# Halving the units of the weighted values, adding four of them by DMA, and copying attention weights with one DMA per chunk

## The chip, the cores and the metric

One core of a Trainium2 chip runs the kernel. The metric is the device time of one execution in microseconds (us), the median over several runs. A profiled run also has a span, from its first to its last recorded instruction, which is about 2 us shorter than the time. A run counts as slow when it is over 1.5% above the fastest of its kernel, and as fast otherwise; all comparisons below are between fast runs. In one group of rounds a single run of the kernel before was slow (218.4 us, granted clock 0.76); it enters no ratio. The granted clock is the share of full speed at which the chip let the tensor engine run. A DMA "lands" when the last of its sixteen completions is recorded.

## The reference, cut to what matters

```python
# A: local attention. 2048 tokens, 512 features, 32 heads of 16, 8 positions at distance 0, 2, ..., 14
logits = einsum("bhsd,bhswd->bhsw", q, kg) * scale        # 8 logits for each token and head
attn   = softmax(where(mask, logits, -1e9))
o      = einsum("bhsw,bhswd->bhsd", attn, vg)             # the weighted values
a      = o.reshape(B, S, D) @ wo
# B: a token mixer: layernorm, then two matrix products over the tokens, with a gelu between
b      = (gelu(layernorm(x)^T @ w1 + b1) @ w2 + b2)^T
out    = g * a + (1 - g) * b                              # g = sigmoid(x . gate_w)
```

The weighted values are the part that changes: for each of 2048 x 512 outputs, 8 products and 7 additions, elementwise, on the vector engine (DVE), while the tensor engine (PE) computes part B beside it. The projection with `wo` needs the weighted values and is added into the same PSUM banks as the last product of B.

## The kernel before

The kernel records operations in a small scheduler, which fixes the order of each engine's instructions before the launch; engines then run in that order and wait on semaphores. `A(engine, function, duration, ...)` records an operation, `tt` is one DVE instruction over two tensors, `sch.dma` is one DMA, and `prio` and the durations only steer the order.

Attention weights of one half of the tokens lie in `ATT[h]`: 128 partitions = 4 chunks of 256 tokens x 32 heads. The weighted values need them on 128 partitions = 32 heads x 4 groups of the head's features. So each chunk (32 partitions of 4 KB) is copied four times, to every fourth partition, by four DMAs of 128 KB:

```python
for c in range(4):
    for dhi in range(4):
        src = psub(ATT[h], 32 * c, 32, 0, [(1, NW * UT_)])
        dst = bass.AP(AVW[h].tensor, AVW[h].offset + dhi * pst + c * NW * UT_, [[4 * pst, 32], [1, NW * UT_]])
        prev = sch.dma("pool", ..., 131072, ds, issue=1.0, reads=["att%d" % h], writes=["avw%d_%d_%d" % (h, c, dhi)] + al, ...)
```

Then eight units of 256 tokens: one product of 8192 elements a partition, and three additions that halve it to 1024:

```python
for u in range(8):
    h, c = u // 4, u % 4
    pv = PV[1 if u % 2 == 0 else 0]                       # two buffers
    A("dve", tt(pv, <values>, <weights of chunk c>, ALU.mult), 4.42, ..., name="avm%d" % u)
    A("dve", tt(pv[:, 0:4], pv[:, 0:4], pv[:, 4:8], ALU.add), 2.28, ..., name="ava%d" % u)
    A("dve", tt(pv[:, 0:2], pv[:, 0:2], pv[:, 2:4], ALU.add), 1.22, ..., name="avb%d" % u)
    avl = A("dve", tt(OT[:, u], pv[:, 0], pv[:, 1], ALU.add), 0.68, ..., name="avc%d" % u)
```

The end of the kernel is a row of sixteen output tiles of 128 tokens. Each takes 14 matmuls of part B, four of the projection (`wo`, which reads `OT`), an eviction on ScalarE (ACT) that needs the small vectors `OMG` (a reciprocal on DVE) and `C2`, and a DMA out. The projections trail by five tiles.

Of the kernel before, what the change touches and what calls it, by code (L numbers as in the profile page):

```python
# [8 lines left out]
ALU = mybir.AluOpType  # L9
AF = mybir.ActivationFunctionType  # L10
# [3 lines left out]
D = 512  # L14
NH = 32
DH = 16
NW = 8
# [290 lines left out]
def bass_gated_mix__sliding_local_dilated__mixer_token_mlp__prompt_kernel(nc, A_x, A_wqkv, A_wo, B_x, B_w1, B_b1, B_w2, B_b2, gate_w, out, dbg=None):  # L308
    with contextlib.ExitStack() as es:
# [128 lines left out]
        def sub(ap_, offs, dims):  # L438
            return bass.AP(ap_.tensor, ap_.offset + offs, [list(ap_.ap[0])] + [list(d) for d in dims])

        def psub(ap_, p0, np_, offs, dims):
            pst = ap_.ap[0][0]
            return bass.AP(ap_.tensor, ap_.offset + p0 * pst + offs, [[pst, np_]] + [list(d) for d in dims])

        def tt(o_, a_, b_, op_):
            return lambda e: e.tensor_tensor(out=o_, in0=a_, in1=b_, op=op_)  # L446

        def act(o_, i_, f_, **kw):
            return lambda e: e.activation(out=o_, in_=i_, func=f_, **kw)  # L449
# [99 lines left out]
        def PE(fn, dur, reads, writes, name, prio=0):  # L549
            op = A("pe", fn, dur, reads=reads, writes=writes, after=([chain[0]] if chain[0] is not None else []), name=name, prio=prio)  # L550
            chain[0] = op
            return op
# [174 lines left out]
        for h in range(2):  # L727
            for pr in range(2):
                bb = PLAN[h][pr]
                for k_ in range(2):  # L730
                    dl = 2 * pr + k_
                    for s_, n_ in (((0, 512), (512, 512)) if h == 0 else ((0, HS),)):
                        sbs = [2 * h + x_ for x_ in range(s_ // 512, (s_ + n_) // 512)]
                        A("dve", tt(sub(PB[bb[k_]], s_, [(HS, NW), (1, n_)]), sub(QH[h], dl * HS + s_, [(0, NW), (1, n_)]),
                                    sub(KH[h], dl * KR + PAD + s_, [(-2, NW), (1, n_)]), ALU.mult), 4.32 * n_ / HS + 0.1,
                          reads=["q%d_%d" % (dl, x_) for x_ in sbs] + ["k%d_%d" % (dl, x_) for x_ in sbs] + (["khalo"] if h else ["kpad"] if s_ == 0 else ["k%d_0" % dl]),
                          writes=PR[bb[k_]], name="qk%d_%d_%d" % (h, dl, s_))
                A("dve", tt(PB[bb[0]], PB[bb[0]], PB[bb[1]], ALU.add), 4.42, reads=PR[bb[1]], writes=PR[bb[0]], name="qa%d_%d" % (h, pr))
            b0, b1 = PLAN[h][0][0], PLAN[h][1][0]
            A("pe", f_sum(h, b0, b1, h == 0), 2.1 + (1.0 if h == 0 else 0), reads=PR[b0] + PR[b1] + ["rp"] + ((XTALL + ["gwrep"]) if h == 0 else []),  # L740
              writes=LGB + (["b3"] if h == 0 else []), name="sum%d" % h, prio=-100, delay=0.5)
            if h == 0:
                A("act", act(E32, ps[:, 3, :], AF.Relu, scale=-1.0, bias=ZMAX), 0.6, reads=["b3"], writes=["e32"], name="zclip")
                A("act", act(EB, E32, AF.Exp, scale=-1.0, bias=ZMAX), 0.6, reads=["e32"], writes=["eb"], name="zexp", table=LOGEXP)
            A("act", act(LOG[h], ps[:, 4:8, :], AF.Copy), 1.9, reads=LGB, writes=["log%d" % h], name="lev%d" % h, prio=-5)
            if h == 0:
                A("dve", tt(psub(LOG[0], 0, 32, 0, [(UT_, NW), (1, PAD)]), psub(LOG[0], 0, 32, 0, [(UT_, NW), (1, PAD)]), MASK, ALU.add), 0.2,
                  reads=["mask"], writes=["log0"], name="msk")
            TR = ["s4", "s2", "s1"]
            A("dve", tt(M4, LOG[h][:, 0:4, :], LOG[h][:, 4:8, :], ALU.max), 0.65, reads=["log%d" % h], writes=["s4"], name="mx4_%d" % h)  # L750
            A("dve", tt(M2, M4[:, 0:2, :], M4[:, 2:4, :], ALU.max), 0.4, reads=["s4"], writes=["s2"], name="mx2_%d" % h)
            A("dve", tt(M1, M2[:, 0, :], M2[:, 1, :], ALU.max), 0.25, reads=["s2"], writes=["s1"], name="mx1_%d" % h)
            A("dve", tt(LOG[h], LOG[h], sub(M1, 0, [(0, NW), (1, UT_)]), ALU.subtract), 1.2, reads=["s1"], writes=["log%d" % h], name="msub%d" % h)
            A("act", act(ATT[h], LOG[h], AF.Exp), 1.9, reads=["log%d" % h], writes=["att%d" % h], name="exp%d" % h, prio=-5, table=LOGEXP)
            A("dve", tt(S4, ATT[h][:, 0:4, :], ATT[h][:, 4:8, :], ALU.add), 1.2, reads=["att%d" % h], writes=["s4"], name="sm4_%d" % h)
            A("dve", tt(S2, S4[:, 0:2, :], S4[:, 2:4, :], ALU.add), 0.65, reads=["s4"], writes=["s2"], name="sm2_%d" % h)
            A("dve", tt(S1, S2[:, 0, :], S2[:, 1, :], ALU.add), 0.4, reads=["s2"], writes=["s1"], name="sm1_%d" % h)
            A("act", act(RS, S1, AF.Ln), 0.4, reads=["s1"], writes=["rs"], name="lns%d" % h, prio=-5, table=LOGEXP)
            A("dve", tt(RS, RS, E32[:, h * UT_:(h + 1) * UT_], ALU.add), 0.35, reads=["e32"], writes=["rs"], name="rsz%d" % h)
            A("act", act(RB, RS, AF.Exp, scale=-1.0, bias=ZMAX), 0.4, reads=["rs"], writes=["rb"], name="rb%d" % h, prio=-5, table=LOGEXP)  # L760
            A("dve", tt(ATT[h], ATT[h], sub(RB, 0, [(0, NW), (1, UT_)]), ALU.mult), 1.2, reads=["rb"], writes=["att%d" % h], name="nrm%d" % h)
            al = ["q%d_%d" % (dl, 2 * h + s_) for dl in range(4) for s_ in range(2)] + ["k%d_%d" % (dl, 2 * h + s_) for dl in range(4) for s_ in range(2)]
            al += ["khalo"] if h else ["kpad"]
            prev = None
            for c in range(4):
                for dhi in range(4):
                    src = psub(ATT[h], 32 * c, 32, 0, [(1, NW * UT_)])
                    pst = AVW[h].ap[0][0]
                    dst = bass.AP(AVW[h].tensor, AVW[h].offset + dhi * pst + c * NW * UT_, [[4 * pst, 32], [1, NW * UT_]])
                    ds = sch.dsem("av%d_%d_%d" % (h, c, dhi))  # L770
                    prev = sch.dma("pool", (lambda d_, s_: lambda e: e.dma_start(d_, s_))(dst, src), 131072, ds, issue=1.0,  # L771
                                   reads=["att%d" % h], writes=["avw%d_%d_%d" % (h, c, dhi)] + al, after=[prev] if prev else [],
                                   name="av%d_%d_%d" % (h, c, dhi))
                    al = []

        def f_te(e):
            ins = None
# [7 lines left out]
        A("dve", tt(C2, OMG, B2C, ALU.mult), 0.12, reads=["omg", "b2c"], writes=["c2"], name="c2")  # L785


        avl = None
        for u in range(8):
            h, c = u // 4, u % 4  # L790
            b = 1 if u % 2 == 0 else 0
            pv = PV[b]
            vr = ["v%d_%d" % (dl, sb) for dl in range(4) for sb in sorted(set([u // 2, max(0, (256 * u - PAD)) // 512]))]
            A("dve", tt(pv, sub(V5, PAD + 256 * u, [(-2, NW), (VR, 4), (1, UT_)]), sub(AVW[h], c * NW * UT_, [(UT_, NW), (0, 4), (1, UT_)]), ALU.mult), 4.42,
              reads=["avw%d_%d_%d" % (h, c, dhi) for dhi in range(4)] + vr + ["vpad"], writes=["p%d" % b], after=[avl] if avl else [], name="avm%d" % u)
            A("dve", tt(pv[:, 0:4], pv[:, 0:4], pv[:, 4:8], ALU.add), 2.28, writes=["p%d" % b], name="ava%d" % u)
            A("dve", tt(pv[:, 0:2], pv[:, 0:2], pv[:, 2:4], ALU.add), 1.22, writes=["p%d" % b], name="avb%d" % u)
            avl = A("dve", tt(OT[:, u], pv[:, 0], pv[:, 1], ALU.add), 0.68, reads=["p%d" % b], writes=["ot%d" % u, OTRES[u]], name="avc%d" % u)


        def f_ph2(ft, bank, half):
# [46 lines left out]

        def finish_tile(i):
            bank = banks[i]  # L850
            PE(f_wo(i, bank, 0, D), 0.87, ["ot%d" % (i // 2), "wo"], ["b%d" % bank], "wo%d" % i)
            A("act", act(OUTS[:, i % 4, :], ps[:, bank, :], AF.Identity, scale=col(OMG, i), bias=col(C2, i)), 0.78,
              reads=["b%d" % bank, "omg", "c2"], writes=["outs%d" % (i % 4)] + (["p2h"] if i == 0 else []), name="ev%d" % i)
            sch.dma("sp", (lambda i_: lambda e: e.dma_start(outv[:, i_, :], OUTS[:, i_ % 4, :]))(i), 131072, ds_out[i % 4], issue=0.5,
                    reads=["outs%d" % (i % 4)], name="d_out%d" % i)
# [17 lines left out]
            finish_tile(i)  # L873
        for hf, (c0, c1) in enumerate(CH):
            bank = lastb[hf]
            PE(f_wo(L, bank, c0, c1), 0.44, ["ot%d" % (L // 2), "wo"], ["b%d" % bank], "wo%d_%d" % (L, hf))
            if hf == 0:
                A("act", act(OUTS[:, 4, c0:c1], ps[:, bank, 0:256], AF.Identity, scale=col(OMG, L), bias=col(C2, L)), 0.55,
                  reads=["b%d" % bank, "omg", "c2"], writes=["outs4"], name="ev%da" % L)
# [86 lines left out]
```

## Time and profile before

171.09 us, median of three runs (170.79 to 171.18). The profiled run has a span of 168.5 us.

| | before |
|---|---|
| PE busy | 161.6 us (96%) |
| DVE busy | 151.9 us (90%) |
| first product of weighted values starts | 88.24 us |
| last addition ends | 163.9 us |
| PE idle before its last projections | 1.04 us |

The first part of the page gives each engine's busy time, share of the span and number of instructions:

```profile
span 168.5 us, 2085 instructions
PE 161.6 (96%) x835; PEld 79.4 (47%) x851; DVE 151.9 (90%) x115; ACT 73.1 (43%) x102; POOL 19.6 (12%) x57
```

Two engines are nearly full, so shares alone do not say which one ends the kernel. PE's timeline does; its columns are start, length, engine, line, operation, and in brackets the idle time ahead and what ended it. L832 is part B, L841 the projection:

```profile
156.46 3.22 PE L832 MATMUL ps<-arena 128*128 128x256 bf16 x28
159.51 3.62 PE L841 MATMUL ps<-arena 128*128 128x512 bf16 x16
164.18 1.69 PE L841 MATMUL ps<-arena 128*128 128x512 bf16 x11 [1.04 <-DVE arena L446]
```

PE runs through until 163.1 us, waits 1.04 us for DVE, and does the last twelve matmuls (one is missing from the trace). The end of the chain of waits (start, length, what) shows what DVE was doing: one unit after another, the last one here. Steps called "issue" of 0.02 us stand between the rows and are left out.

```profile
154.56 5.04 DVE arena L446 x2
159.62 2.30 DVE arena L446
161.94 1.24 DVE arena L446
163.20 0.70 DVE arena L446
163.91 0.27 issue
164.18 1.70 PE ps L841 x11
```

The groups of DVE instructions by form, from 87.2 us on (count, busy us, mean ns, idle before), give the price of each size:

```profile
L446 DVE TENSOR_TENSOR arena<-arena 128x8192 bf16<-128x8192 bf16 x8 | 35.4, 4419 | 0.9 <-DMA arena<-arena 0.9
L446 DVE TENSOR_TENSOR arena<-arena 128x4096 bf16<-128x4096 bf16 x8 | 18.3, 2290 | 0.2
L446 DVE TENSOR_TENSOR arena<-arena 128x2048 bf16<-128x2048 bf16 x10 | 12.1, 1223 | 0.3
L446 DVE TENSOR_TENSOR arena<-arena 128x1024 bf16<-128x1024 bf16 x9 | 6.2, 691 | 0.3
```

DVE's timeline where the first product starts, and the attention copies (number, length of one issue in ns, first and last start; then issue to landing):

```profile
86.92 0.25 DVE L784 RECIPROCAL arena<-arena 128x16 f32<-128x16 f32 x1
87.21 0.17 DVE L446 TENSOR_TENSOR arena<-arena 128x16 f32<-128x16 f32 x1
88.24 5.03 DVE L446 TENSOR_TENSOR arena<-arena 128x8192 bf16<-128x8192 bf16 x2 [0.85 <-DMA arena<-arena]
...
L771 POOL DMA_DIRECT2D arena<-arena x32: 511/519/535, 83.0 to 118.1; - x32
...
DMA to landing us min/median/max: 2.9/4.3/8.4
```

The first of the four DMAs of the first chunk is issued at 82.97 us, the fourth lands at 88.11 us, and DVE waited 0.85 us for it.

### The profile page before, as it was taken

The numbers are of one execution on the slowest core, as the hardware profiler recorded it, in microseconds if no ns is written. First come the engines' busy times: TensorE is split into PE (matmuls) and PEld (weight loads), VectorE is DVE, ScalarE is ACT, GpSimd is POOL, SyncE is SP. The second block draws the span as 40 slices with busy tenths as digits, with TensorE's granted clock in tenths as the row PEclk, the third lists the DMA queues.
The fourth block names the chain that finished last, engine by engine and source line by source line (L and its number), as shares of the span: only waits on it lengthen the run. The fifth ranks groups of instructions, "written<-read, shape, count | busy, mean of one in ns | idle before, by whom it ended". The sixth has DMA issues, their size and how long they took to land.

```text
span 168.5 us, 2085 instructions
## 1 busy us (share of the span) xinstructions
PE 161.6 (96%) x835; PEld 79.4 (47%) x851; DVE 151.9 (90%) x115; ACT 73.1 (43%) x102; POOL 19.6 (12%) x57
## 2 busy tenths in 40 slices
PE   6999999999989999999999999999999999999973
PEld 2865555555534444444443444444444444444732
DVE  2609999999999799999979999999999999999981
ACT  3266777666671277656215297000121111111172
POOL 7000000000000000000396000079100000000000
PEclk9999999999999999999999999999999999999999
DMA  5999999910000392995799999999900011000022
GB/s 137 271 247 252 235 321 290 302 66 6 0 0 0 110 302 63 285 286 142 215 218 288 355 275 270 290 243 207 198 31 31 31 46 51 31 31 31 31 91 96
DMA packets 43144, 26.87 MB, mean 159 GB/s; under 512 B 7552, under 2 KB 41984, under 8 KB 43136
## 3 DMA queue, kind: packets, MB, share of 16 engines
q1 hardware_dynamic: 40800, 21.96, 49.9%
q0 software_dynamic: 1632, 4.21, 10.4%
q10 hardware_dynamic: 704, 0.59, 1.1%
q8 instruction: 6, 0.10, 0.3%
q14 instruction: 2, 0.02, 0.0%
HBM read 18.88 MB, written 2.10 MB: 125 GB/s over the span
## 4 chain that ended last, share of the span: by engine, by line
PE 54%; DVE 36%; ACT 4%; issue 3%; DMA 2%; DVEq 0%
DVE arena L446 36%; PE ps L805 24%; PE ps L649 22%; ACT arena L449 3%; PE ps L590 2%; PE ps L719 2%; DMA arena<-in_A_x_dram 2%; PE ps L841 1%; PE ps L569 1%; ACT L901 1%; PE ps L713 1%; PE ps L560 1%; DVE arena L881 0%; DVEq L905 0%; PE ps L779 0%
## 5 line engine op out<-in xcount | busy, mean ns | idle before, releaser
L446 DVE TENSOR_TENSOR arena<-arena 128x8192 bf16<-128x8192 bf16 (+10 forms) x72 | 134.8, 1902 | 3.2 <-DMA arena<-arena 0.9
L832 PE MATMUL ps<-arena 128*128 128x512 bf16 (+1 forms) x234 | 50.0, 366 | 0.2
L805 PE MATMUL ps<-arena 128*128 128x512 bf16 x218 | 48.7, 379 | 1.4 <-ACT arena L449 0.8
L449 ACT ACTIVATE arena<-ps,arena 128x512 bf16<-128x512 f32 (+1 forms) x30 | 21.6, 728 | 65.2 <-PE ps L841 46.6
L449 ACT ACTIVATE arena<-ps 128x512 bf16<-128x512 f32 (+3 forms) x53 | 33.4, 649 | 20.3 <-PE ps L649 10.4
L649 PE MATMUL ps<-arena 128*128 128x512 bf16 x172 | 38.0, 379 | 0.2
L832 PEld LDWEIGHTS ps<-arena 128*128 128x128 bf16 x238 | 23.3, 98 | 25.3
L805 PEld LDWEIGHTS ps<-arena 128*128 128x128 bf16 x224 | 21.5, 98 | 28.2 <-ACT arena L449 1.8
L649 PEld LDWEIGHTS ps<-arena 128*128 128x128 bf16 x176 | 19.8, 113 | 17.7
L771 POOL DMA_DIRECT2D arena<-arena x32 | 16.4, 517 | 98.3 <-DVE arena L446 98.3
L688 DVE BATCH_NORM_STATS2 arena<-arena 128x6 f32<-128x512 bf16 x16 | 10.0, 682 | 7.5 <-DMA arena<-in_A_x_dram 7.5
L841 PE MATMUL ps<-arena 128*128 128x512 bf16 (+1 forms) x66 | 15.5, 366 | 1.1 <-DVE arena L446 1.0
L901 ACT ACT_TABLE_LOAD x9 | 11.5, 1283 | 2.4 <-issue 2.3
L841 PEld LDWEIGHTS ps<-arena 128*128 128x128 bf16 x68 | 6.6, 98 | 8.2 <-DVE arena L446 1.3
L449 ACT ACTIVATE arena<-arena 128x16 f32<-128x16 f32 (+5 forms) x10 | 6.8, 679 | 5.2 <-DVE arena L446 5.1
L702 DVE TENSOR_SCALAR arena<-arena 128x512 bf16<-128x512 bf16 x16 | 5.3, 413 | 0.0
L590 PE MATMUL ps<-arena 128*128 128x256 bf16 x32 | 3.8, 273 | 0.0
L719 PE MATMUL ps<-arena 128*32 128x512 bf16 x64 | 3.8, 380 | 0.0
L590 PEld LDWEIGHTS ps<-arena 128*128 128x128 bf16 x32 | 3.4, 114 | 0.4 <-DVE arena L580 0.4
L543 PE MATMUL ps<-arena 128*128 128x512 bf16 x5 | 2.3, 628 | 1.1 <-POOL arena L455 1.1
L719 PEld LDWEIGHTS ps<-arena 128*32 128x32 bf16 x64 | 1.6, 97 | 1.9 <-issue 0.4
L881 DVE TENSOR_SCALAR arena<-ps,arena 128x256 bf16<-128x256 f32 x1 | 0.5, 544 | 2.0 <-PE ps L841 2.0
(36 smaller groups left out, 15.3 us busy)
## 6 DMA issues: line engine op xcount, KB each, us to landing
arena<-in_B_w_dram SPq DMA_DIRECT2D x7, 1024.0 KB, 8.3
arena<-in_B_w_dram SPq DMA_DIRECT2D x8, 896.0 KB, 7.9
arena<-arena POOLq DMA_DIRECT2D x32, 128.0 KB, 4.3
out_dram<-arena SPq DMA_DIRECT2D x15, 128.0 KB, 1.7
arena<-in_A_x_dram SPq DMA_DIRECT2D x3, 512.0 KB, 4.3
arena<-in_A_wqkv_dram SPq DMA_DIRECT2D x2, 512.0 KB, 5.9
arena<-in_A_wo_dram SPq DMA_DIRECT2D x1, 512.0 KB, 8.7
arena<-in_A_x_dram SPq DMA_DIRECT2D x2, 128.0 KB, 3.4
```

Of the source, the lines that this page charges most:

```text
L446: return lambda e: e.tensor_tensor(out=o_, in0=a_, in1=b_, op=op_)
L449: return lambda e: e.activation(out=o_, in_=i_, func=f_, **kw)
L590: ins = e.matmul(ps[:, dl, hb * 256:hb * 256 + 256], lhsT=sub(WQKV, dt * 3 * D + dl, [(4, 128)]), rhs=XT[:, dt, hb * 256:hb * 256 + 256], ...
L649: ins = e.matmul(ps[:, bank, :], lhsT=sub(WQKV, dt * 3 * D + tn * D + dl, [(4, 128)]), rhs=XT[:, dt, sb * 512:(sb + 1) * 512], start=(dt = ...
L688: A("dve", (lambda t_: lambda e: e.bn_stats(out=ST6[:, t_, :], in_=X[:, t_, :]))(t), 0.67, reads=["x%d" % t], writes=["st%d" % t], name="s ...
L702: A("dve", (lambda t_: lambda e: e.tensor_scalar(out=X[:, t_, :], in0=X[:, t_, :], scalar1=col(RSTD, t_), scalar2=col(NMR, t_), op0=ALU.mu ...
L719: ins = e.matmul(ps[32 * c:32 * c + 32, 4 + wp, :], lhsT=RP, rhs=sub(PB[b_], 2 * wp * HS + c * UT_, [(HS, 2), (1, UT_)]), start=(k_ == 0), ...
L771: prev = sch.dma("pool", (lambda d_, s_: lambda e: e.dma_start(d_, s_))(dst, src), 131072, ds, issue=1.0, reads=["att%d" % h], writes=["av ...
L805: ins = e.matmul(ps[:, bank, :], lhsT=W1W[:, (ft // 2) % 3, st, 128 * (ft % 2):128 * (ft % 2) + 128], rhs=X[:, st, :], start=(st == 0), st ...
L832: ins = e.matmul(ps[:, bank, 0:c1 - c0], lhsT=W2S[i // 2][:, ft, 128 * (i % 2):128 * (i % 2) + 128], rhs=UT[:, ft, c0:c1], start=(ft == 0) ...
L841: ins = e.matmul(ps[:, bank, 0:c1 - c0], lhsT=OT[:, i // 2, dl, 128 * (i % 2):128 * (i % 2) + 128], rhs=WO[:, dl, c0:c1], start=False, sto ...
L901: e.preload_act_table_set(want)
```

## The change

Its intent: units of 128 tokens in four buffers, so that DVE can start a unit while another is still being reduced; for four of the sixteen units the first, largest addition is taken from DVE and done by a DMA that accumulates into SBUF; and one DMA per chunk in place of four for the attention copies. The softmax operations get a stronger priority, which keeps their place in the order.

```diff
-                for dhi in range(4):
-                    src = psub(ATT[h], 32 * c, 32, 0, [(1, NW * UT_)])
-                    dst = bass.AP(AVW[h].tensor, AVW[h].offset + dhi * pst + c * NW * UT_, [[4 * pst, 32], [1, NW * UT_]])
-                    prev = sch.dma("pool", ..., 131072, ds, issue=1.0, ...)
+                src = psub(ATT[h], 32 * c, 32, 0, [(0, 4), (1, NW * UT_)])
+                dst = sub(AVW[h], c * NW * UT_, [(1, NW * UT_)])
+                prev = sch.dma("pool", ..., 524288, sch.dsem("av%d_%d" % (h, c)), issue=1.0, ...)
 ...
-        for u in range(8):                # product 4.42, additions 2.28, 1.22, 0.68, in two buffers
+        AVD = (6, 8, 10, 12)
+        def av_mult(i):                   # four buffers: slot = i % 4
+            AV(tt(pv, <values>, <weights>, ALU.mult), 2.27, ...)
+            if i in AVD:
+                sch.dma("pool", ... e.dma_start(pw(0, 4), pw(4, 4), accum_op=ALU.add), 1500000, ..., name="avd%d" % i)
+        def av_add(i):
+            if i not in AVD:
+                AV(tt(pw(0, 4), pw(0, 4), pw(4, 4), ALU.add), 1.14, ...)
+            AV(tt(pw(0, 2), pw(0, 2), pw(2, 2), ALU.add), 0.62, ...)
+            AV(tt(<OT of 128 tokens>, pw(0, 1), pw(1, 1), ALU.add), 0.36, ...)
+        for i in range(16):               # a unit added by DMA is finished on DVE two units later
+            av_mult(i); ...
 ...
-            PE(f_wo(i, bank, 0, D), 0.87, ["ot%d" % (i // 2), "wo"], ...)
+            PE(f_wo(i, bank, 0, D), 0.87, ["ot%d" % i, "wo"], ...)
 ...           (and prio=-30 on the softmax operations)
```

PE, ACT and SP keep their order of instructions. On DVE the order of the weighted values changes, and `C2`, which stood right behind the reciprocal, moves to the middle of the units.

More of the change, by code (lines that the diff above doesn't have):

```diff
@@ L744, in bass_gated_mix__sliding_local_dilated__mixer_token_mlp__prompt_kernel @@
                 A("act", act(EB, E32, AF.Exp, scale=-1.0, bias=ZMAX), 0.6, reads=["e32"], writes=["eb"], name="zexp", table=LOGEXP)
-            A("act", act(LOG[h], ps[:, 4:8, :], AF.Copy), 1.9, reads=LGB, writes=["log%d" % h], name="lev%d" % h, prio=-5)
+            A("act", act(LOG[h], ps[:, 4:8, :], AF.Copy), 1.9, reads=LGB, writes=["log%d" % h], name="lev%d" % h, prio=-30)
             if h == 0:
                 A("dve", tt(psub(LOG[0], 0, 32, 0, [(UT_, NW), (1, PAD)]), psub(LOG[0], 0, 32, 0, [(UT_, NW), (1, PAD)]), MASK, ALU.add), 0.2,
-                  reads=["mask"], writes=["log0"], name="msk")
+                  reads=["mask"], writes=["log0"], name="msk", prio=-30)
@@ L749, in bass_gated_mix__sliding_local_dilated__mixer_token_mlp__prompt_kernel @@
             TR = ["s4", "s2", "s1"]
-            A("dve", tt(M4, LOG[h][:, 0:4, :], LOG[h][:, 4:8, :], ALU.max), 0.65, reads=["log%d" % h], writes=["s4"], name="mx4_%d" % h)
-            A("dve", tt(M2, M4[:, 0:2, :], M4[:, 2:4, :], ALU.max), 0.4, reads=["s4"], writes=["s2"], name="mx2_%d" % h)
-            A("dve", tt(M1, M2[:, 0, :], M2[:, 1, :], ALU.max), 0.25, reads=["s2"], writes=["s1"], name="mx1_%d" % h)
-            A("dve", tt(LOG[h], LOG[h], sub(M1, 0, [(0, NW), (1, UT_)]), ALU.subtract), 1.2, reads=["s1"], writes=["log%d" % h], name="msub%d" % h)
@@ L754, in bass_gated_mix__sliding_local_dilated__mixer_token_mlp__prompt_kernel @@
-            A("act", act(ATT[h], LOG[h], AF.Exp), 1.9, reads=["log%d" % h], writes=["att%d" % h], name="exp%d" % h, prio=-5, table=LOGEXP)
-            A("dve", tt(S4, ATT[h][:, 0:4, :], ATT[h][:, 4:8, :], ALU.add), 1.2, reads=["att%d" % h], writes=["s4"], name="sm4_%d" % h)
-            A("dve", tt(S2, S4[:, 0:2, :], S4[:, 2:4, :], ALU.add), 0.65, reads=["s4"], writes=["s2"], name="sm2_%d" % h)
-            A("dve", tt(S1, S2[:, 0, :], S2[:, 1, :], ALU.add), 0.4, reads=["s2"], writes=["s1"], name="sm1_%d" % h)
@@ L758, in bass_gated_mix__sliding_local_dilated__mixer_token_mlp__prompt_kernel @@
-            A("act", act(RS, S1, AF.Ln), 0.4, reads=["s1"], writes=["rs"], name="lns%d" % h, prio=-5, table=LOGEXP)
-            A("dve", tt(RS, RS, E32[:, h * UT_:(h + 1) * UT_], ALU.add), 0.35, reads=["e32"], writes=["rs"], name="rsz%d" % h)
-            A("act", act(RB, RS, AF.Exp, scale=-1.0, bias=ZMAX), 0.4, reads=["rs"], writes=["rb"], name="rb%d" % h, prio=-5, table=LOGEXP)
-            A("dve", tt(ATT[h], ATT[h], sub(RB, 0, [(0, NW), (1, UT_)]), ALU.mult), 1.2, reads=["rb"], writes=["att%d" % h], name="nrm%d" % h)
+            A("dve", tt(M4, LOG[h][:, 0:4, :], LOG[h][:, 4:8, :], ALU.max), 0.65, reads=["log%d" % h], writes=["s4"], name="mx4_%d" % h, prio=-30)
@@ new lines, in bass_gated_mix__sliding_local_dilated__mixer_token_mlp__prompt_kernel @@
+            A("dve", tt(M2, M4[:, 0:2, :], M4[:, 2:4, :], ALU.max), 0.4, reads=["s4"], writes=["s2"], name="mx2_%d" % h, prio=-30)
+            A("dve", tt(M1, M2[:, 0, :], M2[:, 1, :], ALU.max), 0.25, reads=["s2"], writes=["s1"], name="mx1_%d" % h, prio=-30)
+            A("dve", tt(LOG[h], LOG[h], sub(M1, 0, [(0, NW), (1, UT_)]), ALU.subtract), 1.2, reads=["s1"], writes=["log%d" % h], name="msub%d" % h, prio=-30)
+            A("act", act(ATT[h], LOG[h], AF.Exp), 1.9, reads=["log%d" % h], writes=["att%d" % h], name="exp%d" % h, prio=-30, table=LOGEXP)
@@ new lines, in bass_gated_mix__sliding_local_dilated__mixer_token_mlp__prompt_kernel @@
+            A("dve", tt(S4, ATT[h][:, 0:4, :], ATT[h][:, 4:8, :], ALU.add), 1.2, reads=["att%d" % h], writes=["s4"], name="sm4_%d" % h, prio=-30)
+            A("dve", tt(S2, S4[:, 0:2, :], S4[:, 2:4, :], ALU.add), 0.65, reads=["s4"], writes=["s2"], name="sm2_%d" % h, prio=-30)
+            A("dve", tt(S1, S2[:, 0, :], S2[:, 1, :], ALU.add), 0.4, reads=["s2"], writes=["s1"], name="sm1_%d" % h, prio=-30)
+            A("act", act(RS, S1, AF.Ln), 0.4, reads=["s1"], writes=["rs"], name="lns%d" % h, prio=-30, table=LOGEXP)
@@ L762, in bass_gated_mix__sliding_local_dilated__mixer_token_mlp__prompt_kernel @@
+            A("dve", tt(RS, RS, E32[:, h * UT_:(h + 1) * UT_], ALU.add), 0.35, reads=["e32"], writes=["rs"], name="rsz%d" % h, prio=-30)
+            A("act", act(RB, RS, AF.Exp, scale=-1.0, bias=ZMAX), 0.4, reads=["rs"], writes=["rb"], name="rb%d" % h, prio=-30, table=LOGEXP)
+            A("dve", tt(ATT[h], ATT[h], sub(RB, 0, [(0, NW), (1, UT_)]), ALU.mult), 1.2, reads=["rb"], writes=["att%d" % h], name="nrm%d" % h, prio=-30)
             al = ["q%d_%d" % (dl, 2 * h + s_) for dl in range(4) for s_ in range(2)] + ["k%d_%d" % (dl, 2 * h + s_) for dl in range(4) for s_ in range(2)]
@@ L765, in bass_gated_mix__sliding_local_dilated__mixer_token_mlp__prompt_kernel @@
             for c in range(4):
-                for dhi in range(4):
-                    src = psub(ATT[h], 32 * c, 32, 0, [(1, NW * UT_)])
-                    pst = AVW[h].ap[0][0]
-                    dst = bass.AP(AVW[h].tensor, AVW[h].offset + dhi * pst + c * NW * UT_, [[4 * pst, 32], [1, NW * UT_]])
-                    ds = sch.dsem("av%d_%d_%d" % (h, c, dhi))
-                    prev = sch.dma("pool", (lambda d_, s_: lambda e: e.dma_start(d_, s_))(dst, src), 131072, ds, issue=1.0,
-                                   reads=["att%d" % h], writes=["avw%d_%d_%d" % (h, c, dhi)] + al, after=[prev] if prev else [],
-                                   name="av%d_%d_%d" % (h, c, dhi))
-                    al = []
+                src = psub(ATT[h], 32 * c, 32, 0, [(0, 4), (1, NW * UT_)])
+                dst = sub(AVW[h], c * NW * UT_, [(1, NW * UT_)])
+                prev = sch.dma("pool", (lambda d_, s_: lambda e: e.dma_start(d_, s_))(dst, src), 524288, sch.dsem("av%d_%d" % (h, c)), issue=1.0,
+                               reads=["att%d" % h], writes=["avw%d_%d" % (h, c)] + al, after=[prev] if prev else [], name="av%d_%d" % (h, c))
+                al = []
         def f_te(e):
@@ L785, in bass_gated_mix__sliding_local_dilated__mixer_token_mlp__prompt_kernel @@
         A("dve", tt(C2, OMG, B2C, ALU.mult), 0.12, reads=["omg", "b2c"], writes=["c2"], name="c2")
-        avl = None
-        for u in range(8):
-            h, c = u // 4, u % 4
-            b = 1 if u % 2 == 0 else 0
-            pv = PV[b]
-            vr = ["v%d_%d" % (dl, sb) for dl in range(4) for sb in sorted(set([u // 2, max(0, (256 * u - PAD)) // 512]))]
-            A("dve", tt(pv, sub(V5, PAD + 256 * u, [(-2, NW), (VR, 4), (1, UT_)]), sub(AVW[h], c * NW * UT_, [(UT_, NW), (0, 4), (1, UT_)]), ALU.mult), 4.42,
-              reads=["avw%d_%d_%d" % (h, c, dhi) for dhi in range(4)] + vr + ["vpad"], writes=["p%d" % b], after=[avl] if avl else [], name="avm%d" % u)
-            A("dve", tt(pv[:, 0:4], pv[:, 0:4], pv[:, 4:8], ALU.add), 2.28, writes=["p%d" % b], name="ava%d" % u)
-            A("dve", tt(pv[:, 0:2], pv[:, 0:2], pv[:, 2:4], ALU.add), 1.22, writes=["p%d" % b], name="avb%d" % u)
-            avl = A("dve", tt(OT[:, u], pv[:, 0], pv[:, 1], ALU.add), 0.68, reads=["p%d" % b], writes=["ot%d" % u, OTRES[u]], name="avc%d" % u)
+        AVD = (6, 8, 10, 12)
@@ new lines, in bass_gated_mix__sliding_local_dilated__mixer_token_mlp__prompt_kernel, with AV, av_parts @@
+        avlast = [None]
+        def AV(fn, dur, **kw):
+            avlast[0] = A("dve", fn, dur, after=[avlast[0]] if avlast[0] else [], **kw)
+        def av_parts(i):
+            slot = i % 4
+            pv = sub(PB[1 - slot // 2], (slot % 2) * 4096, [(512, NW), (128, 4), (1, 128)])
+            return "av%d" % slot, pv, (lambda w0, nw: sub(pv, w0 * 512, [(1, nw * 512)]))
+        def av_mult(i):
+            h, u = i // 8, i // 2
+            res, pv, pw = av_parts(i)
+            vr = ["v%d_%d" % (dl, sb) for dl in range(4) for sb in sorted(set([i // 4, max(0, (128 * i - PAD)) // 512]))]
+            AV(tt(pv, sub(V5, PAD + 128 * i, [(-2, NW), (VR, 4), (1, 128)]),
+                  sub(AVW[h], (u % 4) * NW * UT_ + 128 * (i % 2), [(UT_, NW), (0, 4), (1, 128)]), ALU.mult), 2.27,
+               reads=["avw%d_%d" % (h, u % 4)] + vr + ["vpad"],
+               writes=[res] + (PR[1 - (i % 4) // 2] if i < 4 else []), name="avm%d" % i)
+            if i in AVD:
+                sch.dma("pool", (lambda o_, i_: lambda e: e.dma_start(o_, i_, accum_op=ALU.add))(pw(0, 4), pw(4, 4)), 1500000, sch.dsem("avd%d" % i), issue=1.0,
+                        writes=[res], name="avd%d" % i)
@@ new lines, in av_add @@
+        def av_add(i):
+            u = i // 2
+            res, pv, pw = av_parts(i)
+            if i not in AVD:
+                AV(tt(pw(0, 4), pw(0, 4), pw(4, 4), ALU.add), 1.14, writes=[res], name="ava%d" % i)
+            AV(tt(pw(0, 2), pw(0, 2), pw(2, 2), ALU.add), 0.62, writes=[res], name="avb%d" % i)
+            AV(tt(sub(OT, u * 4 * UT_ + 128 * (i % 2), [(UT_, 4), (1, 128)]), pw(0, 1), pw(1, 1), ALU.add), 0.36,
+               reads=[res], writes=["ot%d" % i] + ([OTRES[u]] if i % 2 == 0 else []), name="avc%d" % i)
@@ L801, in f_ph2 @@
+        todo = []
+        for i in range(NST):
+            av_mult(i)
+            if todo and todo[0] + 2 <= i:
+                av_add(todo.pop(0))
+            if i in AVD:
+                todo.append(i)
+            else:
+                av_add(i)
         def f_ph2(ft, bank, half):
@@ L850, in finish_tile @@
             bank = banks[i]
-            PE(f_wo(i, bank, 0, D), 0.87, ["ot%d" % (i // 2), "wo"], ["b%d" % bank], "wo%d" % i)
+            PE(f_wo(i, bank, 0, D), 0.87, ["ot%d" % i, "wo"], ["b%d" % bank], "wo%d" % i)
             A("act", act(OUTS[:, i % 4, :], ps[:, bank, :], AF.Identity, scale=col(OMG, i), bias=col(C2, i)), 0.78,
@@ L875, in bass_gated_mix__sliding_local_dilated__mixer_token_mlp__prompt_kernel @@
             bank = lastb[hf]
-            PE(f_wo(L, bank, c0, c1), 0.44, ["ot%d" % (L // 2), "wo"], ["b%d" % bank], "wo%d_%d" % (L, hf))
+            PE(f_wo(L, bank, c0, c1), 0.44, ["ot%d" % L, "wo"], ["b%d" % bank], "wo%d_%d" % (L, hf))
             if hf == 0:
```

## The prediction

> What bounds it now. The page gives PE 96% busy (161.6 of 168.5 us) and DVE 90%; the granted clock is 1.0. The slices show PE at nine or ten tenths from start-up to the last two slices, so PE is the floor and DVE is almost as long. The chain of waits ends in DVE: from 99.7 us it is one row of DVE pieces, unit after unit of weighted values (8.64 us each: 4.43 + 2.30 + 1.23 + 0.62 and short gaps), to the last addition at 163.9 us. PE's timeline shows what this costs: its output projections run through 163.1 us, then it idles 1.04 us for DVE and does the last twelve matmuls until 165.87 us. So a faster DVE can win about 1.1 us at most; all other PE waits together are under a few tenths after start-up.
>
> What changes on DVE (durations from the groups by form). Before, 8 units of 8192, 4096, 2048 and 1024 elements: 4.42 + 2.29 + 1.22 + 0.69 = 8.62 us, 69 us in all. After, 16 units of 4096, 2048, 1024 and 512: 2.29 + 1.22 + 0.69 + 0.42 = 4.63 us, 74 us; halving costs 5 us of fixed time, because 8192 elements take 4.42 us but two times 4096 take 4.58. Four first additions (1.22 us each, 4.9 us) leave DVE. So DVE work stays about the same: 69.1 against 69.0 us. What is gained is overlap (two independent pairs per 256 tokens instead of one, about 0.08 us each) and grain: the last projections but one no longer wait for a unit of 256 tokens. Replaying the new order by hand with the trace's start-to-start times, from the first weighting at 88.2 us as before, the last addition ends at 163.0 us, 0.9 us earlier, and PE needs it at 163.8 us. PE then runs without the 1.04 us wait, and ends about 1.15 us earlier.
>
> The accumulating DMA is the risk. It reads 512 KB twice and writes it once. DVE reaches its result about 6.7 us after the first issue and 7.8 us after the other three. Copies in the trace land first 2.3 us after issue and move a 4 KB packet in 160 to 340 ns on each engine. The Trainium skill ("Collectives: The Full Stack", The bandwidth ceiling) says that an add in the DMA needs two source reads, which halves the rate; no run here shows it yet. My estimate from both: 8 packets per engine at 320 to 680 ns, plus 2.3, plus up to 1 us for four times the descriptors: 5 to 8.7 us. At 8 us the stalls (1.3 + 3 x 0.2 us) eat all but a little of the gain; at 9 us the kernel loses about 4 us; at 10 us about 8 us.
>
> The attention copies: 32 DMAs of 128 KB (16.4 us of POOL) become 8 of 512 KB. Before, DVE waited 0.85 us for the first chunk, landing at 88.1 us; one DMA of the same bytes should land within 0.7 us of that. The rest have over 10 us of slack. POOL's saving is off the path.
>
> Predicted: 170.1 us, range 169.5 to 173.0. Faster by over 2%: 2%. Within 2%: 83%. Slower by over 2%: 15%.
>
> Right if: PE's wait before the last projections is gone or under 0.3 us, DVE's busy time is within 1 us, DVE's waits for DMA stay under 1.5 us, accumulations land in under 7.5 us, PE busy unchanged. Wrong if: accumulations land after 8 us (DVE then waits at the four second additions, and the end moves), descriptor generation is slowed beside busy DVE, or the first copy lands late.

## The result, and the profile after

171.05 us, median of four runs (170.70 to 171.24), against 170.97 us of the kernel before in the same rounds. The ratio is 1.0002, with a 95% interval of 0.998 to 1.0024: no change. (A ratio here is the mean time of one kernel's fast runs over that of the other's of the same rounds, so it is not quite the ratio of the medians.)

| | before | after |
|---|---|---|
| PE busy | 161.6 us | 161.9 us |
| DVE busy | 151.9 us | 150.6 us |
| first product of weighted values starts | 88.24 us | 90.46 us |
| last addition ends | 163.9 us | 165.2 us |
| PE idle before its last projections | 1.04 us | 0.78 us |

```profile
span 168.9 us, 2078 instructions
PE 161.9 (96%) x835; PEld 78.9 (47%) x851; DVE 150.6 (89%) x143; ACT 72.9 (43%) x102; POOL 11.1 (7%) x37
```

PE's timeline at the end, in the changed kernel (L859 is part B, L868 the projection). All but the last tile's projection now run through, as intended, yet PE still waits for DVE, and later:

```profile
156.93 3.22 PE L859 MATMUL ps<-arena 128*128 128x256 bf16 x28
159.99 4.48 PE L868 MATMUL ps<-arena 128*128 128x512 bf16 x19
165.24 1.05 PE L868 MATMUL ps<-arena 128*128 128x256 bf16 x8 [0.78 <-DVE arena L446]
```

The end of its chain of waits is DVE's last unit, of 128 tokens (steps of 0.02 us left out again):

```profile
162.77 1.24 DVE arena L446
164.03 0.70 DVE arena L446
164.76 0.44 DVE arena L446
165.19 0.05 issue
165.24 1.06 PE ps L868 x8
```

The groups of DVE instructions by form from 87.2 us on are what the prediction had added up: 16 products, 12 first additions (the other two of 2048 elements belong to the softmax), and the waits for DMA stand at one place, before a product:

```profile
L446 DVE TENSOR_TENSOR arena<-arena 128x4096 bf16<-128x4096 bf16 x16 | 36.5, 2285 | 3.1 <-DMA arena<-arena 3.1
L446 DVE TENSOR_TENSOR arena<-arena 128x2048 bf16<-128x2048 bf16 x14 | 16.9, 1222 | 0.3
L446 DVE TENSOR_TENSOR arena<-arena 128x1024 bf16<-128x1024 bf16 x17 | 11.7, 689 | 0.4
L446 DVE TENSOR_TENSOR arena<-arena 128x512 bf16<-128x512 bf16 x17 | 7.2, 426 | 0.6
```

DVE's timeline shows that it is the first product of all, and the DMA issues show both kinds of DMA (L768 the attention copies, L805 the additions):

```profile
87.07 0.24 DVE L780 RECIPROCAL arena<-arena 128x16 f32<-128x16 f32 x1
90.46 3.55 DVE L446 TENSOR_TENSOR arena<-arena 128x4096 bf16<-128x4096 bf16 x2 [3.14 <-DMA arena<-arena]
...
L768 POOL DMA_DIRECT2D arena<-arena x8: 535/564/582, 83.1 to 115.9; - x8
...
DMA to landing us min/median/max: 6.6/10.5/14.5
...
L805 POOL DMA_DIRECT2D arena<-arena x4: 852/871/939, 126.9 to 149.5; - x4
...
DMA to landing us min/median/max: 4.5/4.6/4.8
```

The copy of the first chunk is issued at 83.12 us and lands at 90.33 us, 7.2 us later. The four DMAs of before brought the same bytes in 5.1 us. DVE therefore starts the weighted values 2.2 us later than before (2.1 us when both are counted from the reciprocal just ahead). It has no other wait for a DMA behind it, and the last addition ends 2.2 us later than the replay of the prediction had it (165.2 against 163.0). The additions by DMA, which the prediction feared, land in 4.5 to 4.8 us, well before DVE needs them.

A second, smaller trace of the change: the evictions need `C2`, which DVE now computes at 128.69 us. ACT sits idle until 128.89 us, releases the first banks late, and PE pauses about 0.3 us near 129.5 us.

My theory after this: the single 512 KB copy of the first chunk lands late, and this alone hides a gain of about 1 us. Rivals: the smaller DVE operations or the additions by DMA eat the gain; `C2` does; or the late landing has another cause than the form of the copy.

### The profile page after: what moved, and what is told of

Read it like the earlier page. It is cut to its first block, busy times and chain, and to the rows that moved or that the text cites. A ratio compares the mean times of both kernels' runs of the same rounds, so it can differ in the third digit from the quotient of the medians.

```text
span 168.9 us, 2078 instructions
## 1 busy us (share of the span) xinstructions
PE 161.9 (96%) x835; PEld 78.9 (47%) x851; DVE 150.6 (89%) x143; ACT 72.9 (43%) x102; POOL 11.1 (7%) x37
## 4 chain that ended last, share of the span: by engine, by line
DVE 57%; PE 30%; DMA 7%; issue 4%; SPq 0%; ACT 0%; DVEq 0%
DVE arena L446 55%; PE ps L649 22%; DMA arena<-arena 4%; PE ps L832 4%; DMA arena<-in_A_x_dram 3%; PE ps L590 1%; PE ps L719 1%; DVE arena L688 1%; PE ps L868 1%; PE ps L713 1%; SPq L486 0%; ACT arena L449 0%; DVE arena L908 0%; DVE arena L580 0%; PE ps L662 0%
## 5 line engine op out<-in xcount | busy, mean ns | idle before, releaser
L446 DVE TENSOR_TENSOR arena<-arena 128x4096 bf16<-128x4096 bf16 (+9 forms) x100 | 133.5, 1370 | 6.7 <-DMA arena<-arena 3.1
L859 PE MATMUL ps<-arena 128*128 128x512 bf16 (+1 forms) x234 | 50.0, 366 | 0.4
L859 PEld LDWEIGHTS ps<-arena 128*128 128x128 bf16 x238 | 23.2, 98 | 25.7 <-ACT arena L449 0.6
L868 PE MATMUL ps<-arena 128*128 128x512 bf16 (+1 forms) x66 | 15.7, 366 | 0.9 <-DVE arena L446 0.8
L768 POOL DMA_DIRECT2D arena<-arena x8 | 4.3, 563 | 108.1 <-DVE arena L446 108.1
L868 PEld LDWEIGHTS ps<-arena 128*128 128x128 bf16 x68 | 6.6, 98 | 8.2 <-DVE arena L446 1.3
L805 POOL DMA_DIRECT2D arena<-arena x4 | 3.5, 883 | 30.4 <-DVE arena L446 30.4
```

The lines of the kernel that those rows point to most:

```text
L446: return lambda e: e.tensor_tensor(out=o_, in0=a_, in1=b_, op=op_)
L768: prev = sch.dma("pool", (lambda d_, s_: lambda e: e.dma_start(d_, s_))(dst, src), 524288, sch.dsem("av%d_%d" % (h, c)), issue=1.0, reads= ...
L859: ins = e.matmul(ps[:, bank, 0:c1 - c0], lhsT=W2S[i // 2][:, ft, 128 * (i % 2):128 * (i % 2) + 128], rhs=UT[:, ft, c0:c1], start=(ft == 0) ...
L868: ins = e.matmul(ps[:, bank, 0:c1 - c0], lhsT=OT[:, i // 2, dl, 128 * (i % 2):128 * (i % 2) + 128], rhs=WO[:, dl, c0:c1], start=False, sto ...
```

## The experiments

Profiled runs reach this stage at slightly different times: the reciprocal that stands just ahead of the weighted values starts between 86.92 us (before) and 87.99 us (e2). In e1 an early load lands 0.9 us later than before; in e2 that load does not, and the cause of its shift was not looked for. So the table counts from the start of the reciprocal. All kernels gave the right result except m1 and m2. m1 and m2 have two runs each; they are there for their landing times.

| kernel | first product | last addition | PE ends | median us | ratio to before (95% interval) |
|---|---|---|---|---|---|
| before | 1.32 | 76.97 | 78.94 | 170.97 | |
| after | 3.39 | 78.11 | 79.22 | 171.05 | 1.0002 (0.998 to 1.0024) |
| e1 old copies | 1.33 | 76.06 | 77.95 | 169.64 | 0.9904 (0.9884 to 0.9923) |
| e2 new copies alone | 2.99 | 78.32 | 80.29 | 172.89 | 1.0097 (1.0069 to 1.0125) |
| e3 old copies, C2 early | 1.38 | 76.23 | 77.95 | 169.81 | 0.9932 (0.9896 to 0.9968) |
| e7 C2 early | 3.37 | 78.22 | 79.33 | 171.18 | 0.9997 (0.9964 to 1.003) |
| e4 first chunk split | 1.82 | 76.66 | 77.95 | 170.10 | 0.9922 (0.9897 to 0.9947) |
| e5 no additions by DMA | 1.41 | 81.91 | 83.85 | 175.52 | 1.0249 (1.0222 to 1.0277) |
| e6 a fifth addition, early | 1.71 | 80.46 | 81.95 | 172.99 | 1.0102 (1.0058 to 1.0145) |
| e8 a fifth addition, late | 1.58 | 74.91 | 77.95 | 169.56 | 0.9899 (0.9873 to 0.9925) |
| m1 plain source | 0.16 | 74.87 | 77.94 | 170.02 | 0.9922 (0.9883 to 0.9961) |
| m2 four pieces | 3.58 | 78.30 | 79.41 | 171.36 | 1.0001 (0.9961 to 1.004) |

### e1: the changed kernel with the copies of before

```diff
-                src = psub(ATT[h], 32 * c, 32, 0, [(0, 4), (1, NW * UT_)])
-                dst = sub(AVW[h], c * NW * UT_, [(1, NW * UT_)])
-                prev = sch.dma(..., 524288, ..., issue=1.0, ...)
+                for dhi in range(4):
+                    src, dst = <as before>
+                    prev = sch.dma(..., 131072, ds, issue=0.25, ...)
```

The issue weight of 0.25 keeps the scheduler's order on every other engine exactly that of the changed kernel.

> The changed kernel with the sixteen 128 KB copies per half back; order on DVE, ACT, PE and SP exactly that of the changed kernel. My theory (the single 512 KB copy of the first chunk lands late and moves the whole DVE chain): first weighting starts at 88.2 to 88.5 us instead of 90.5, last addition ends at 163.0 us (+-0.3) instead of 165.2, PE does not wait before the last projection, time about 169.9 us (1.1 us or 0.65% under before). Rival (the gain is eaten by the smaller operations, the accumulating DMAs or the late C2): last addition still at 165 us, 171.0 us.

Measured: 169.64 us, ratio 0.9904. The first product starts 1.33 us after the reciprocal, as before, and the last addition ends at 76.06 us on the same count; the prediction's replay, 163.0 less 86.92, had 76.08. DVE's first product, and PE, which has no wait left at the end:

```profile
89.08 4.28 DVE L446 TENSOR_TENSOR arena<-arena 128x4096 bf16<-128x4096 bf16 x3 [1.08 <-DMA arena<-arena]
157.29 3.22 PE L863 MATMUL ps<-arena 128*128 128x256 bf16 x28
160.35 5.35 PE L872 MATMUL ps<-arena 128*128 128x512 bf16 x28
```

So the rest of the change does bring what was predicted; the copies took it back. The absolute times in the expectation (163.0 us) were missed by the 0.8 us that this run was late at the reciprocal.

### e2: the kernel before with the new copies alone

```diff
+                src = psub(ATT[h], 32 * c, 32, 0, [(0, 4), (1, NW * UT_)])
+                dst = sub(AVW[h], c * NW * UT_, [(1, NW * UT_)])
+                prev = sch.dma(..., 524288, ..., issue=4.0, ...)      # in place of the four DMAs
```

(With prio=-30 on the softmax operations, so that the order stays that of before.)

> The kernel before with only the attention copies changed to one 512 KB DMA per chunk (scheduler weights set so that the order on every other engine is that of before). My theory: first chunk lands about 7.2 us after its issue instead of 5.1, first weighting at 90.3 to 90.6 us, everything behind it 2.1 us later, 173.1 us (+1.2%). Rival (the late landing belongs to something else of the change): first weighting at 88.2 us, 171.0 us.

Measured: 172.89 us, ratio 1.0097, where +1.2% was expected. The first chunk takes 6.8 us, the first product starts 1.67 us later than before, and PE ends 1.35 us later (80.29 against 78.94). The times differ by 1.6 us (171.31 us before in the same rounds), and five of the six runs (not the profiled one) show a granted clock of 0.986 to 0.99; what that adds was not separated.

```profile
90.98 4.43 DVE L446 TENSOR_TENSOR arena<-arena 128x8192 bf16<-128x8192 bf16 x1 [2.52 <-DMA arena<-arena]
```

The rival that something else of the change makes the chunk land late is out. The copies alone cost; with e1 the loss is shown from both sides.

### e3 and e7: C2 early, with the old and with the new copies

```diff
-  A("dve", tt(C2, OMG, B2C, ALU.mult), 0.12, ..., name="c2")
+  A("dve", tt(C2, OMG, B2C, ALU.mult), 0.12, ..., name="c2", prio=-30)
```

> As e1, and the small product C2 done early again, as before. Theory: PE is the floor, so the same time as e1 within 0.2 us (about 169.9 us); the first output stage no longer waits until 126 us. Rival (C2 late is part of the loss): e3 is 0.3 us or more faster than e1.

> The changed kernel with C2 early and nothing else. Theory: PE's pause of 0.3 us near 129.5 us goes, but the DVE chain ends the kernel, so the time stays at 171.0 us (+-0.2) and PE's wait before the last projection grows from 0.8 to 1.1 us. Rival (PE's pause is on the path): 170.7 us.

Measured: e3 169.81 us, e7 171.18 us, intervals overlapping those of e1 and of the changed kernel. In e7 PE's pause near 129.5 us is gone, and PE's wait before the last projection grows from 0.78 to 1.21 us. The late `C2` costs nothing while DVE ends the kernel: here PE gives the pause back at the end. e3 against e1 does not test the pause, because e1 has none: with the first product on time its `C2` comes at 127.32 us, and PE does not wait for it.

### e4: only the first chunk in four DMAs

```diff
+                if (h, c) == (0, 0):
+                    <four DMAs of 128 KB, as before>
+                    continue
                 src = psub(ATT[h], 32 * c, 32, 0, [(0, 4), (1, NW * UT_)])
```

(and C2 early. On DVE the scheduler also moves operations of the second half's softmax forward, so that the second half's copies are issued from 109.8 us on, against 113.7 us in e7.)

> The changed kernel with C2 early and only the very first chunk of attention copied by four 128 KB DMAs; the other seven chunks stay one 512 KB DMA each. Theory (only the first chunk is waited for): first weighting 1.3 to 1.5 us after the reciprocal, DVE waits for no other copy, time as e1 and e3, 169.7 us (ratio to before 0.990 to 0.994). Rival (the slower later copies are waited for too): 170.5 us or more.

Measured: 170.10 us, ratio 0.9922. The other seven chunks land 7.6 to 15.8 us after issue, and DVE waits for none of them. The first product starts 1.82 us after the reciprocal, a little later than expected: its fourth DMA took 4.1 us here. PE ends at 77.95 as in e1. Only the first chunk is on the path; the changed kernel says the same, where DVE waits for a DMA among the weighted values only once (3.14 us).

### e5: no additions by DMA

```diff
-        AVD = (6, 8, 10, 12)
+        AVD = ()
```

(in e3.)

> As e3 (old copies, C2 early), but no addition by DMA: the sixteen 128-token units all add on DVE. Theory (the DMA additions pay for the cost of halving the units): four first additions come back, 4 x 1.38 us of DVE, last addition 5.5 us later than in e3, about 174.2 us (+1.9% on before; +2.6% on e3). Rival (the DMA additions bring nothing because DVE or POOL pay for them elsewhere): within 0.5 us of e3, 169.8 us.

Measured: 175.52 us, ratio 1.0249, 3.4% over e3's median. The last addition comes 5.7 us later than in e3 on the table's count, near the 5.5 expected. The time grew 1.3 us more than expected, and part of it is the clock. Windows of the last stage, the first two overlapping (length, busy time of PE, PEld, DVE, ACT, POOL, then the granted clock, DMA share, GB/s):

```profile
163.40:166.80 3.40, 1.10 (x5) 0.31 (x4) 3.33 (x4) 1.80 (x3) 0.00 (x0) 1.00 0.33 116
165.00:169.40 4.40, 0.81 (x3) 0.20 (x2) 4.29 (x4) 0.78 (x1) 0.00 (x0) 0.70 0.17 60
169.40:171.40 2.00, 1.89 (x8) 1.04 (x8) 0.03 (x1) 0.56 (x1) 0.00 (x0) 0.50 0.00 0
```

PE waited 1.33 and 3.61 us for DVE, the granted clock fell to 0.50, and the last eight matmuls took 1.89 us, where the changed kernel needs 1.05. The Trainium skill ("TensorE: Matmul & The Clock Gate", Part 1: The HAM clock gate) gives half the clock after an idle window of about 3.4 us. This run agrees on the half, but no idle stretch of 3.4 us came before it: the mean of 0.70 over 165.0 to 169.4 us puts the fall at about 166.8 us, 1.0 us into the second wait, and PE had worked 1.1 us in the 3.4 us before that. So without the DMA additions the smaller units are a loss, and here PE's last wait cost 0.84 us more than its length.

### e6 and e8: a fifth addition by DMA

```diff
-        AVD = (6, 8, 10, 12)
+        AVD = (4, 6, 8, 10, 12)        # e6
+        AVD = (6, 8, 10, 12, 13)       # e8
```

(both in e3.)

> As e3, with five instead of four units added by DMA. Theory (PE is the floor): DVE's last addition comes 1.4 us earlier relative to its first weighting than in e3, and the time stays as e3, 169.7 us +-0.3. Rival (DVE still on the path): 168.5 us.

> As e3, with a fifth unit added by DMA, but the thirteenth instead of the fourth, so that no DMA addition is issued among the attention copies (which is what held e6's first addition 8.1 us). Theory (PE is the floor once DVE is early): all five additions land in under 5.5 us, the last addition comes 1.2 to 1.4 us earlier after the first weighting than in e3, and the time is e3's, 169.7 us +-0.3. Rival (DVE still on the path): 168.5 us.

e6 was meant to show that PE is the floor and failed at that: 172.99 us, neither of the two expectations. Its first addition stands on the queue right behind the sixteen copies of the second half, is issued at 119.57 us while those copies land until 125.2 us, and lands 8.1 us after its issue; DVE stands still for it:

```profile
127.72 3.35 DVE L446 TENSOR_TENSOR arena<-arena 128x1024 bf16<-128x1024 bf16 x3 [5.20 <-DMA arena<-arena]
```

e8 puts the fifth addition after the copies. All five land within 4.6 us, the last addition ends 1.3 us earlier than in e3 on the table's count (74.91 against 76.23; 1.5 us earlier counted from the first product), and PE still ends at 77.95. Five kernels with DVE's last addition anywhere from 74.9 to 76.7 end PE at 77.94 or 77.95: that is PE's own work, and a faster DVE brings nothing more. The median, 169.56 us, is the lowest, but its interval overlaps those of e1, e3 and e4.

### m1 and m2: why the single copy is slow

Both write wrong weights and keep all instructions, sizes and destinations of the changed kernel; only the source differs.

```diff
-                src = psub(ATT[h], 32 * c, 32, 0, [(0, 4), (1, NW * UT_)])
+                src = sub(ATT[h], 0, [(1, NW * UT_)])                       # m1: 128 partitions, once
+                src = psub(V5, 32 * c, 32, 0, [(VR, 4), (1, NW * UT_)])     # m2: 32 partitions, four different pieces
```

> Wrong result on purpose. The changed kernel, each attention copy still one 512 KB DMA, but from all 128 partitions of the half once instead of from 32 partitions four times. If the form of the source (32 partitions, each sent to four) is what makes the single copy slow: first chunk lands 5.1 us after issue or sooner, engines ending within 1 us, time about 170 us. If the size of the single DMA is: 7 us and 171.0 us as the changed kernel.

> Wrong result on purpose. As m1, but the source is 32 partitions with four different 4 KB pieces of each (from the values) instead of the same 4 KB four times. If reading the same bytes again is what costs: first chunk lands in 5.1 us or less. If it is that 32 source partitions feed 128 rows in this order: 7 us, engines ending 2.5 us or more apart, as in the changed kernel.

Measured, DMA issue to landing over the eight copies, m1 first, then m2:

```profile
L768 POOL DMA_DIRECT2D arena<-arena x8: 527/527/562, 83.7 to 113.2; - x8
...
DMA to landing us min/median/max: 4.0/5.1/6.4
```

```profile
L768 POOL DMA_DIRECT2D arena<-arena x8: 535/562/585, 83.7 to 116.6; - x8
...
DMA to landing us min/median/max: 6.9/10.5/13.9
```

In m1 the first chunk is there 4.0 us after issue and its 16 completions come within 0.5 us; DVE does not wait at all, and PE ends at 77.94. In m2 it takes 7.4 us, with completions 2.9 us apart; in the changed kernel it was 7.2 us and 2.8 us. So neither the size of the DMA nor reading the same bytes again makes it slow; what is left is the form, 32 source partitions that feed 128 rows in one DMA. m1 changes three things of this form at once: a partition is read once and not four times, consecutive rows come from different partitions, and every row stays on its own partition. These were not told apart. The four DMAs of before also read only 32 partitions and move rows to other partitions, and they took 5.1 us, so those two properties alone do not make 7.2 us.

The packets agree (means over half microseconds, worked out from the packet records of the traces). In the second half, when few loads run beside them, 4 KB packets of m1 take 160 to 175 ns; those of the changed kernel's first copy average 460 to 630 ns in their first 2 us. The DMAs of before, which each read the 32 partitions once, are in between, at 230 to 420 ns. Why the packets take longer is not shown: the trace does not say which engine or port carried a packet.

## Why the prediction was right or wrong

The prediction was 170.1 us, a gain of 0.9 to 1.0 us; the gain was nil. That 171.05 us lies inside the range is luck: the range reached up that far for the additions by DMA, which did no harm here.

- **Wrong, and the step that failed:** "one DMA of the same bytes should land within 0.7 us of that", that is of 88.1 us. It landed at 90.33 us, 2.2 us late. The prediction did list "the first copy lands late" among what would make it wrong, but its sum had no term for it. The step assumed that the same bytes from the same source take the same time in one DMA as in four. The runs show 6.6 to 7.6 us for the first chunk of a half in this form (changed kernel, e2, e4, e7, m2) against 5.0 to 5.7 us in four pieces (before, e1, e3 to e6, e8). e1 undoes it and gains, e2 does it alone and loses.
- **Wrong as a consequence:** "PE's wait before the last projections is gone or under 0.3 us" (0.78 us) and "DVE's waits for DMA stay under 1.5 us" (3.1 us).
- **Right:** PE is the floor and the most to be had is about 1.1 us. PE ends 1.0 us earlier in e1, e3, e4 and e8 on the table's count. In e1's rounds the medians of the spans differ by 1.05 us (169.0 and 167.95); the medians of the times differ by 1.67 us, and the 0.6 us outside the span are not explained.
- **Right:** DVE's work stays the same, because the fixed cost of twice as many instructions equals what four additions save, and the new order would end at 163.0 us. e1 meets this to 0.02 us once counted from the reciprocal. The page's DVE busy time fell by 1.3 us, a little more than the 1 us allowed.
- **Right, the risk wrongly placed:** the additions by DMA land in 4.5 to 4.8 us, just under the 5 to 8.7 us estimated. The estimate's allowance of up to 1 us for descriptors came from no measurement; POOL's issue took 0.35 us longer (0.87 against 0.52). The Trainium skill ("Collectives: The Full Stack", The bandwidth ceiling) explains the half rate of a reduce-scatter by the two source reads that an add needs; here packets of the additions take 328 ns and those of a plain copy (m1) about 160 ns, which agrees. Whole landings differ far less, 4.5 against 4.0 us. What the prediction missed of them is how they fare among other copies: 8.1 and 7.7 us in e6.
- **Not foreseen:** the scheduler moved `C2`; e7 shows that it did not matter here.

## What to carry to other kernels

Before merging DMAs, ask which one the consumer waits for first: merging saves issue time on a queue that may be idle anyway (POOL was 12% busy here), and DVE could not start before the last completion of the single piece (90.33 us, then 90.46). Compare forms of a DMA by their own landing time in the trace, not by bytes. When one engine's work is the floor, work out the most that a relief of the other can bring (here 1 us), since a delay of 2 us in a single first wait is then enough to hide all of it.

## What the Trainium skill lacked or had wrong

- "DMA: Bandwidth & Descriptors", Rules for kernel authors, advises to coalesce many small transfers into one large one; the size that it calls overhead is under 64 KB, and the pieces here had 128 KB. For 32 partitions sent to 128 rows coalescing was slower: 7.2 us in one DMA of 512 KB, 5.1 us in four of 128 KB. The page gives no time for a source that feeds four rows from each partition, and the table of DMA rates by partitions in "SBUF — State Buffer" has no row for it; with 128 partitions on both sides (m1) one DMA took 4.0 us.
- The same page, Anatomy of one DMA, fits a duration of 2.0 us plus bytes over 436e3 per us; by our estimate from it, 3.2 us for 512 KB. The plain copy of m1 (4.0 us from issue) is 0.8 us over it; the 32-to-128 form (6.6 to 7.6 us) is more than twice it.
- No page gives the duration of an accumulating DMA within SBUF. For 128 partitions of 4 KB it is 4.4 to 4.8 us from issue to landing with little else on the queues, of which POOL's issue is 0.85 to 0.94 us (a plain copy's is 0.53 us), and 7.7 and 8.1 us for two that were issued while attention copies were landing (e6). Single ones took 6.3 and 6.4 us (e6, e4) because one completion of sixteen came about 2 us after most others; the runs do not show why.
- "TensorE: Matmul & The Clock Gate", Part 1, does not say how much work a window may hold and still count as idle: in e5 the clock was halved although PE had worked 1.1 us of the 3.4 us before.
